# Attention and softplus MoE on one core: the row maxima of 15 of 16 head pairs turned by VectorE and placed by DMAs instead of turned by TensorE

## The chip, the cores and the metric

The kernel runs on one core of one Trainium2 chip. The time is device microseconds of that core, from a run without a profile; a profiled execution of the same kernel stands beside it. Engines are named as in the profile: PE (TensorE matmul), PEld (its weight loads), DVE (VectorE), ACT (ScalarE), POOL (GpSimd), SP (SyncE, which here only issues DMAs).

## What is computed

```python
def rotate(x):                       # x: 4 batches, 8 heads, 576 positions, 64 wide
    x1, x2 = (x[..., :half], x[..., half:])
    return np.concatenate([x1 * cos - x2 * sin, x1 * sin + x2 * cos], axis=-1)
q_rot, k_rot = (rotate(q), rotate(k))
scores = scale * np.matmul(q_rot, k_rot.transpose(0, 1, 3, 2))
scores = scores - np.max(scores, axis=-1, keepdims=True)
attn = np.exp(scores)
attn = attn / (np.sum(attn, axis=-1, keepdims=True) + 1e-09)
x = (attn @ v), heads side by side   # 2304 x 512
h = x @ w_in                         # 512 x 2048
g = np.maximum(h, 0.0) + np.log1p(np.exp(-np.abs(h)))
out = g @ w_out                      # 2048 x 512
```

All inputs are float32. The kernel splits each operand of a matmul into a high and a low part (`hl`, `kk`, `vs`, `ph` and `pl`, `wh` and `wl`) and adds up three products.

## The kernel before

Attention is done for 16 pairs of heads; the two heads of a pair lie on partitions 0 to 63 and 64 to 127, and every matmul comes twice, once for each half of the rows. The loop in `attention` runs over slots `s`, nine for a pair (`p, r = divmod(s, 9)`; slot r of a pair below). The order of the instructions on each engine is that in which the loop writes them (`pin`), and DMAs issued on SP keep theirs among themselves (`chain`). A slot holds work of several pairs:

- `p1(s)`, for pair p: scores with the queries on the partitions, 128 at a time against 288 keys, into a PSUM bank of the pool `ps_1`, which has one buffer; then DVE takes the negated row maximum of them into `mx` (L489). The last 64 queries of both heads, the corner, are done together, with `qd`, in which the two heads' queries stand in blocks off each other's rows; in all pairs but the first that is slot 5.
- `p2(n2)` with `n2 = s - 10`, so from slot 1 of the next pair on: the scores of the pair before again, now turned (keys on the partitions, 288 queries along the columns), into a bank of `ps_2`, which has two buffers. A fourth pair of matmuls adds the bias: a matrix of ones times `sm`, rows that hold the shift (minus the row maximum) of each query as a high and a low part. In slot 5 `p2c` does the corner keys with `kd`.
- `exps`: ACT takes the exponential twice, into `ph` and back into the bank; `low`: DVE forms `pl` from the two (L564). The loop keeps the bank that `low` used last as `spare`; free columns of it hold scratch values.
- `pv_half`: PE multiplies the probabilities with v, two slots later.

Between `p1` and `p2` the maxima, one to a partition, have to become rows. `shift0` (DVE) joins the two key halves after slots 6 and 8, `shift1` (POOL) makes high and low parts in `sh`, `shift2` (PE) turns them by matmuls with the unit matrix (L515: six in slot 0 of the next pair, for three groups of 128 queries, and four in slot 3), `shift3` (ACT, L522 and L526) copies them from PSUM into `sm`. `corner` copies the corner queries and keys into `qd` and `kd` with two DMAs each, in slots 1 and 8.

Beside this POOL and ACT turn the next pairs' queries and keys (`rope_steps`), and the MoE weights of three of sixteen chunks are converted early, in steps that `PLAN` and `MASKS` place; the steps of `MASKS` are two DVE instructions each (L136, L140) that use `spare`, two steps in slot 4 of twelve pairs. After slot 156 comes the MoE stage (`emit_h`, `emit_o`), 1152 and 864 matmuls and more, on PE without a gap.

Of the kernel before, what the change touches and what calls it, by code (L numbers as in the profile page):

```python
# [44 lines left out]
MASKS = {22 + 9 * n: n // 2 for n in range(12)}  # L45
# [10 lines left out]
def rope_attention_softplus_moe(  # L56
# [250 lines left out]
    def attention(es, es_r, es_s, tail, window, early):  # L307
# [8 lines left out]
        mask = at1.tile([128, 2], F32, name="mask")  # L316
# [15 lines left out]
        nc.vector.memset(sh[0].bitcast(F32), 0.0)  # L332
        flat = sh[0].rearrange("p c x -> p (c x)")
# [108 lines left out]
        order1 = ((*order1, None), (*order1[:5], None, *order1[5:]))  # L442

# [18 lines left out]
        def p1(n, between=None):  # L462
# [11 lines left out]
            if order1[p > 0][r]:  # L474
                c, j = order1[p > 0][r]
                to = m[:, j, c, :]
                for t, (a, b) in enumerate(terms):
                    for i, o in enumerate(rows):
                        pin(nc.tensor.matmul(out=sp[:, i, :HS], lhsT=q[o, a, c * 128:c * 128 + 128],  # L479
                                             rhs=k[o, b, j * HS:(j + 1) * HS], start=(t == 0), stop=(t == 2)))  # L480
            else:
                to = m[:, :, 4, 0]
# [68 lines left out]
        def exps(n, between=None):  # L551
# [3 lines left out]
            if between:  # L555
                between()
# [136 lines left out]
        def first(s):  # L693
# [5 lines left out]
            if n == 3:  # L699
                shift3(0, 1, x)  # L700
# [241 lines left out]
```

## Time and profile before

| | |
|---|---|
| median of 3 runs | 708.74 us (708.55 to 708.76) |
| profiled execution | 708.87 us, its span 706.8 us |
| PE, PEld busy | 698.1 us (99%), 649.3 us (92%) |
| DVE, ACT, POOL busy | 465.0, 388.0, 299.9 us |
| granted TensorE clock | 0.999 |
| attention ends, MoE begins (first `hp` matmul) | 301.2 us |

The span runs from the first to the last instruction. Busy time of PE includes the fill of the pipeline, since matmuls overlap; what a step costs PE is therefore read from the starts of its matmuls in the timeline, not from their durations. A wait is read from the idle time before an instruction and what ended it, and from the list of waits; a wait that ends on an engine with idle time after it costs nothing.

### The profile page before, as it was taken

Reading aid. Unit: us, or ns where it says so; the run is one execution under the profiler, and the core shown is the slowest. Engines: PE = TensorE matmul, PEld = TensorE weight load, DVE = VectorE, ACT = ScalarE, POOL = GpSimd, SP = SyncE. Lnnn points to the kernel's source line nnn. Section 1 sums busy time; section 2 is a strip of 40 time slices with the busy share of each in tenths; the row PEclk is TensorE's granted clock in tenths of the full one; section 3 lists DMA queues with packets and bytes.
Section 4 is the critical chain, followed back from the end, with each engine's and each line's share of the span. In section 5 each row is a group of like instructions: output and inputs, shape, how many; then the busy total and the mean of one; then the engine's idle time right before and its main releaser. Section 6 shows DMA issues by size and latency. Waiting matters only on the chain.

```text
span 706.8 us, 15573 instructions
## 1 busy us (share of the span) xinstructions
PE 698.1 (99%) x6275; PEld 649.3 (92%) x6275; DVE 465.0 (66%) x792; ACT 388.0 (55%) x751; POOL 299.9 (42%) x351
## 2 busy tenths in 40 slices
PE   8999999999999999999999999999999999999997
PEld 7899999999999999899999999999999999999996
DVE  6788888888888877669899894544543343444343
ACT  2788888888888887846766562322222222222222
POOL 7789899889988897820000000730500000000000
PEclk9999999999999999999999999999999999999999
DMA  7444344434454632024424330530100010001001
GB/s 265 147 113 142 112 141 115 141 112 143 138 166 137 167 102 65 19 70 129 138 93 131 108 95 2 177 92 1 68 0 1 1 45 1 1 1 45 1 1 45
DMA packets 40152, 61.33 MB, mean 87 GB/s; under 512 B 14288, under 2 KB 26896, under 8 KB 40080
## 3 DMA queue, kind: packets, MB, share of 16 engines
q1 hardware_dynamic: 37200, 55.16, 26.5%
q10 hardware_dynamic: 2880, 5.18, 2.0%
q8 instruction: 49, 0.80, 0.5%
q14 instruction: 23, 0.19, 0.1%
HBM read 48.64 MB, written 7.23 MB: 79 GB/s over the span
## 4 chain that ended last, share of the span: by engine, by line
PE 88%; DVE 4%; ACT 4%; DMA 2%; issue 1%; POOL 0%; SPq 0%; ACTq 0%; DVEq 0%
PE hp L235 29%; PE oa L274 14%; PE ob L274 14%; PE pv L597 13%; PE sp L549 9%; PE sp L479 6%; PE sp L451 3%; DVE pl L564 2%; ACT sp L557 2%; DVE mx L489 1%; ACT ph L554 1%; PE sp L515 1%; DMA tab<-cs 1%; DMA raw<-qk 0%; DVE sp L136 0%
## 5 line engine op out<-in xcount | busy, mean ns | idle before, releaser
L235 PE MATMUL hp<-x,wh 128*128 128x384 f32 x768 | 196.3, 336 | 0.0
L247 ACT ACTIVATE e<-e 128x384 f32<-128x384 f32 x96 | 50.4, 525 | 203.6 <-DVE e L245 196.5
L235 PEld LDWEIGHTS hp<-x,wh 128*128 128x128 f32 x768 | 140.7, 188 | 8.4 <-issue 0.2
L235 PE MATMUL hp<-x,wl 128*128 128x384 f32 x384 | 129.3, 337 | 0.0
L489 DVE TENSOR_REDUCE mx<-sp 128x2 f32<-128x576 f32 x144 | 108.3, 755 | 31.4 <-PE sp L479 24.3
L597 PE MATMUL pv<-ph,vs 64*128 64x288 f32 (+1 forms) x1152 | 125.2, 296 | 0.5 <-POOL vs L357 0.2
L564 DVE TENSOR_TENSOR pl<-sp,ph 128x576 fp32r<-128x576 f32 x144 | 108.3, 752 | 22.0 <-ACT sm L526 11.2
L554 ACT ACTIVATE ph<-sp 128x576 fp32r<-128x576 f32 x144 | 94.0, 653 | 41.8 <-PE sp L451 21.5
L245 DVE TENSOR_SCALAR e<-hp 128x384 int32<-128x384 int32 x96 | 53.4, 556 | 79.1 <-PE hp L235 79.1
L274 PE MATMUL oa<-wh,g 128*128 128x512 f32 x288 | 97.7, 393 | 0.0
L274 PE MATMUL ob<-wh,g 128*128 128x512 f32 x290 | 97.4, 391 | 0.0
L557 ACT ACTIVATE sp<-sp 128x576 f32<-128x576 f32 x144 | 93.0, 646 | 0.5
L597 PE MATMUL pv<-pl,vs 64*128 64x288 f32 x576 | 87.0, 292 | 0.2 <-DVE pl L564 0.2
L255 DVE TENSOR_TENSOR g<-m,g 128x384 fp32r<-128x384 f32 x96 | 55.8, 581 | 47.0 <-ACT g L252 46.9
L357 POOL TENSOR_TENSOR raw<-raw,tab 128x576 f32<-128x576 f32 x60 | 84.7, 1433 | 2.9 <-DMA raw<-qk 2.9
L250 DVE SCALAR_TENSOR_TENSOR m<-hp,e 128x384 f32<-128x384 f32 x96 | 53.5, 558 | 43.4 <-ACT e L247 42.1
L597 PEld LDWEIGHTS pv<-ph,vs 64*128 64x128 f32 (+1 forms) x1152 | 77.9, 158 | 3.0 <-PE pv L597 0.9
L549 PE MATMUL sp<-hl,kk 64*128 64x288 f32 x768 | 76.7, 302 | 1.1 <-DVE wc L140 0.9
L252 ACT CAST g<-m 128x384 fp32r<-128x384 f32 x96 | 49.3, 513 | 48.6 <-DVE m L250 45.8
L479 PE MATMUL sp<-kk,hl 64*128 64x288 f32 x768 | 73.7, 294 | 0.5 <-DVE kk L357 0.3
L235 PEld LDWEIGHTS hp<-x,wl 128*128 128x128 f32 x384 | 72.0, 188 | 0.0
L274 PEld LDWEIGHTS ob<-wh,g 128*128 128x128 f32 x290 | 54.4, 188 | 10.3
(112 smaller groups left out, 1052.6 us busy)
## 6 DMA issues: line engine op xcount, KB each, us to landing
raw<-qk SPq DMA_DIRECT2D x29, 576.0 KB
wraw<-w SPq DMA_DIRECT2D x23, 512.0 KB
vf<-v SPq DMA_DIRECT2D x16, 320.0 KB
wraw<-w SPq DMA_DIRECT2D x14, 256.0 KB
x<-xt SPq DMA_DIRECT2D x32, 72.0 KB
xd<-xt SPq DMA_DIRECT2D x32, 72.0 KB
x<-rd SPq DMA_DIRECT2D x16, 144.0 KB
out<-wc ACTq DMA_DIRECT2D x9, 256.0 KB
```

Source lines behind the costliest of these rows:

```text
L235: pin(nc.tensor.matmul(out=hp, lhsT=a[f][:, c * 128:(c + 1) * 128], rhs=piece(j, c)[:, b, :], start=(i == 0), stop=(i == 11),))
L250: pin(nc.vector.scalar_tensor_tensor(out=m, in0=hp, scalar=0.0, in1=e, op0=ALU.max, op1=ALU.add))
L255: pin(nc.vector.tensor_tensor(out=g[:, 1, :], in0=m, in1=g[:, 0, :].bitcast(F32), op=ALU.subtract))
L274: pin(nc.tensor.matmul(out=po[:, z], lhsT=g[:, s, t * 128:(t + 1) * 128], rhs=b[f][:, 512 + z.start:512 + z.stop], start=(first and i == 0 ...
L357: pin((nc.vector if e == "V" else nc.gpsimd).tensor_tensor(out=out, in0=in0, in1=in1, op=op))
L479: pin(nc.tensor.matmul(out=sp[:, i, :HS], lhsT=q[o, a, c * 128:c * 128 + 128], rhs=k[o, b, j * HS:(j + 1) * HS], start=(t == 0), stop=(t = ...
L489: pin(nc.vector.tensor_reduce(out=to, in_=sp[:, :, :HS], axis=AX.X, op=ALU.max, negate=True))
L549: pin(nc.tensor.matmul(out=sp[:, i, :HS], lhsT=lhs, rhs=rhs, start=(t == 0), stop=(t == 3)))
L554: pin(nc.scalar.activation(out=ph, in_=sp, func=AF.Exp, scale=D ** -0.5))
L557: pin(nc.scalar.activation(out=sp, in_=sp, func=AF.Exp, scale=D ** -0.5))
L564: pin(nc.vector.tensor_tensor(out=pl, in0=sp[:, :, :HS], in1=ph.bitcast(F32), op=ALU.subtract))
L597: two.append(pin(nc.tensor.matmul(out=pv[:k, i, :HS], lhsT=lhs, rhs=x[o, j if c is None else i, :], start=first, stop=last)))
```

## The change

In all pairs but for the first three groups of pair 0, `shift` does the work of `shift0` to `shift3`. DVE joins the key halves twice, into a scratch place in `spare` and, rounded, into `st`; subtracts for the low part; and turns `st` in blocks of 32 by 32 into `turned`. Then SP issues four DMAs that carry rows of 32 from there to partitions 62 to 65 of `sm` (high and low part, two heads), and two more for a corner. `sm` is cleared once at the start.

The corner queries of pairs 1 to 15 are now queries 256 to 319, not the last 64 (`places`), so the first group of shifts (0 to 319, ready after slot 5) covers the first half of the queries, and the second (320 to 575) is ready after slot 8. `corner` copies with two POOL instructions instead of two DMAs, but for pair 0. The mask steps go from two in slot 4 to one in slot 3 and one in slot 4, and the loads of v from slot 6 to slot 7. The DMAs of a group stand on SP behind the instruction that they wait for, and ahead of the next pair's loads.

```diff
-MASKS = {22 + 9 * n: n // 2 for n in range(12)}
+MASKS = {21 + 9 * n + i: n // 2 for n in range(12) for i in range(2)}
...
-        sh = [at1.tile([128, 5, 128], F32R, name=f"sh{i}") for i in range(2)]
-        sm = [at1.tile([128, 5, 128], F32R, name=f"sm{i}") for i in range(2)]
+        sh = at1.tile([128, 3, 128], F32R, name="sh")
+        sm = [at1.tile([128, S], F32R, name=f"sm{i}") for i in range(2)]
         mx = [at1.tile([128, 2, 5, 2], F32, name=f"mx{i}") for i in range(2)]
-        sf = at1.tile([128, 6, 2], F32, name="sf")
+        st = at1.tile([128, 5, 32], F32R, name="st")
+        turned = [at1.tile([128, 3 - i, 32], F32, name=f"tu{i}") for i in range(2)]
...
-        nc.vector.memset(sh[0].bitcast(F32), 0.0)
-        flat = sh[0].rearrange("p c x -> p (c x)")
+        nc.vector.memset(sh.bitcast(F32), 0.0)
+        for x in (*sm, st):
+            nc.vector.memset(x.bitcast(F32), 0.0)
+        flat = sh.rearrange("p c x -> p (c x)")
...
+            t = t[:, :, 256:320] if p and i == 0 else t[:, :, 512:576]
             for n, o in enumerate(rows):
                 m = 64 * ((n + i) % 2)
-                keep(queue.dma_start(out=x[o, :, m:m + 64].bitcast(F32), in_=t[o, :, 512:].bitcast(F32)))
+                if p:
+                    rnd(x[o, :, m:m + 64], t[o].bitcast(F32), "P")
+                else:
+                    keep(queue.dma_start(out=x[o, :, m:m + 64].bitcast(F32), in_=t[o].bitcast(F32)))
...
+        places = (((0, 0), (128, 1), (256, 2), (384, 3), (512, 4)), ((0, 0), (128, 1), (320, 3), (448, 4), (256, 2)))
...
-        def shift0(p, g):
-            m, cs, to = mx[p % 2], slice(3 * g, 3 + 2 * g), slice(3, 6, 2) if g else slice(0, 3)
-            pin(nc.vector.tensor_reduce(out=sf[:, to], in_=m[:, :, cs].rearrange("p j c a -> p c a j"), axis=AX.X,
-                                        op=ALU.min))
+        def shift(p, g):
+            cs, n = slice(3 * g, 3 + 2 * g), turned[g]
+            m, x = mx[p % 2][:, :, cs].rearrange("p j c a -> p c a j"), st[:, cs]
+            parts = x[:, :, 0:4].rearrange("p c (a h) -> p c a h", h=2)
+            full = spare[0][:, 1, HS:HS + 2 * (3 - g)].rearrange("p (c a) -> p c a", a=2)
+            for to in (full, parts[:, :, :, 0]):
+                pin(nc.vector.tensor_reduce(out=to, in_=m, axis=AX.X, op=ALU.min))
+            tt(parts[:, :, :, 1], full, parts[:, :, :, 0].bitcast(F32), ALU.subtract, "V")
+            pin(nc.vector.transpose(out=n, in_=x.bitcast(F32)))
+            to = sm[p % 2].bitcast(F32)
+            starts = {at: c for c, at in places[p > 0][:4] if cs.start <= at < cs.stop}
+            c0 = min(starts.values())
+            for k in range(4):
+                at = to[62:66, c0:c0 + 128 * len(starts)].rearrange("p (c x) -> p c x", x=128)
+                chain(nc.sync.dma_start(out=at[:, :, 32 * k:32 * k + 32], in_=n[32 * k:32 * k + 4, :len(starts)]))
+            c0 = places[p > 0][4][0]
+            for h in range(2 * (len(starts) < cs.stop - cs.start)):
+                chain(nc.sync.dma_start(out=to[62 + h:66 + h:2, c0:c0 + 64], in_=n[h::32, len(starts)]))
...
-        def shift1(p, g):
-            cs = slice(3 * g, 3 + 2 * g)
-            if g:
-                tt(sf[:, 4, :], sf[:, 5, 0:1].to_broadcast([128, 2]), mask, ALU.mult, "P")
-            x = sh[p % 2].rearrange("p c (a x) -> p c a x", a=2)
-            rnd(x[:, cs, :, 0], sf[:, cs], "P")
-            tt(x[:, cs, :, 1], sf[:, cs], x[:, cs, :, 0].bitcast(F32), ALU.subtract, "P")
-
-        def shift2(p, g, t):
-            for n, c in enumerate((3, 4) if g else range(3)):
+        def shift2(t):
+            for c in range(3):
                 for i, o in enumerate(rows):
-                    pin(nc.tensor.matmul(out=t[:, i, HS + n * 64:HS + n * 64 + 64], lhsT=sh[p % 2][o, c, :],
+                    pin(nc.tensor.matmul(out=t[:, i, HS + c * 64:HS + c * 64 + 64], lhsT=sh[o, c, :],
                                          rhs=identr[o, o], start=True, stop=True))
-            return t[:, :, HS:HS + (128 if g else 192)]
-
-        def shift3(p, g, x):
-            cs = slice(3, 4) if g else slice(0, 3)
-            w = 64 if g else 192
-            pin(nc.scalar.copy(out=sm[p % 2][:, cs, :].rearrange("p c (t x) -> p t c x", t=2),
-                               in_=x[:, :, :w].rearrange("p t (c x) -> p t c x", x=64)))
-            if g:
-                for i, o in enumerate(rows):
-                    pin(nc.scalar.copy(out=sm[p % 2][o, 4, :64], in_=x[o, i, 64:]))
...
-                g = {0: 0, 3: 1}.get(r) if s <= NSLOT + 3 else None
-                x = None if g is None else shift2(p - 1, g, ps2[n2])
                 if r == 5 and s < NSLOT:
                     p1(s, lambda flip, after=(): p2c(n2, flip, after))
                 else:
                     p2(n2)
-                exps(n2, None if g != 0 else (lambda: shift3(p - 1, g, x)))
-                if g == 1:
-                    shift3(p - 1, g, x)
...
-                elif r in (6, 8) and s != 6:
-                    shift0(p, r // 8)
...
             if s in MASKS:
-                for _ in range(2):
-                    next(early[MASKS[s]])
-            if r == 7 and PER < s < NSLOT:
-                shift1(p, 0)
-            if r == 0 and 0 < s <= NSLOT:
-                shift1(p - 1, 1)
+                next(early[MASKS[s]])
+            if r in (5, 8) and 5 < s < NSLOT:
+                shift(p, r // 8)
...
-                if r == 6 and p + 1 < NP:
+                if r == 7 and p + 1 < NP:
                     load_v(p + 1)
```

Where it moves instructions, three places. PE at the beginning of slot 0 of a pair, before:

```order
L597 MATMUL pv<-ph,vs_133 64x288 x2
L597 MATMUL pv<-pl,vs_133 128x288 x2
L515 MATMUL sp_1155<-identr,sh_123 128x64 [waits DVE_49,Pool_49]
L515 MATMUL sp_1155<-identr,sh_123 128x64 x5
L549 MATMUL sp_1155<-hl,kk_100 128x288 x6
L549 MATMUL sp_1155<-sm_126,ones 128x288 x2
```

and after:

```order
L601 MATMUL pv<-ph,vs_133 64x288 x2
L601 MATMUL pv<-pl,vs_133 128x288 x2
L555 MATMUL sp_1164<-hl,kk_100 128x288 [waits DVE_49]
L555 MATMUL sp_1164<-hl,kk_100 128x288 x5
L555 MATMUL sp_1164<-sm_124,ones 128x288 x2
```

The six turning matmuls are gone, and the wait for POOL with them. PE one slot later, at the first `p2` of the next pair (`sp` is the bank, `sm` the shift rows), before:

```order
L549 MATMUL sp_1201<-hl,kk_101 128x288 [waits DVE_49]
L549 MATMUL sp_1201<-hl,kk_101 128x288 x5
L549 MATMUL sp_1201<-sm_125,ones 128x288 [waits Activation_49]
L549 MATMUL sp_1201<-sm_125,ones 128x288
L597 MATMUL pv<-ph,vs_133 128x288 x2
```

and after:

```order
L555 MATMUL sp_1200<-hl,kk_101 128x288 [waits DVE_49]
L555 MATMUL sp_1200<-hl,kk_101 128x288 x5
L555 MATMUL sp_1200<-sm_123,ones 128x288 [waits DMAHW5_49,DMAHW6_49,DMAHW2_49,DMAHW7_49,DMAHW1_49,DMAHW0_49]
L555 MATMUL sp_1200<-sm_123,ones 128x288
L601 MATMUL pv<-ph,vs_133 128x288 [waits Activation_49]
```

The bias matmul waits for the landing of six DMAs where it waited for ACT's copies. DVE from the `low` of slot 4 to that of slot 6, in a pair with mask steps, before:

```order
L564 TENSOR_TENSOR pl<-sp_1725,ph 128x576 [waits Activation_49]
L136 TENSOR_SCALAR sp_1725<-wc 128x128 [waits DVE_49]
L140 SCALAR_TENSOR_TENSOR wc<-wraw,sp_1725 128x128 [waits DMAHW0_49,DVE_49]
L136 TENSOR_SCALAR sp_1725<-wc 128x128 [waits DVE_49]
L140 SCALAR_TENSOR_TENSOR wc<-wraw,sp_1725 128x128 [waits DVE_49]
L489 TENSOR_REDUCE mx_127<-sp_1769 128x2 [waits PE_49]
L564 TENSOR_TENSOR pl<-sp_1768,ph 128x576 [waits Activation_49]
L489 TENSOR_REDUCE mx_127<-sp_1843 128x2 [waits PE_49]
L493 TENSOR_REDUCE sf<-mx_127 128x6 [waits DVE_49,Pool_49]
L564 TENSOR_TENSOR pl<-sp_1818,ph 128x576 [waits Activation_49]
```

and after:

```order
L568 TENSOR_TENSOR pl<-sp_1319,ph 128x576 [waits Activation_49]
L136 TENSOR_SCALAR sp_1319<-wc 128x128 [waits DVE_49]
L140 SCALAR_TENSOR_TENSOR wc<-wraw,sp_1319 128x128 [waits DVE_49]
L497 TENSOR_REDUCE mx_126<-sp_1363 128x2 [waits PE_49]
L568 TENSOR_TENSOR pl<-sp_1362,ph 128x576 [waits Activation_49]
L505 TENSOR_REDUCE sp_1362<-mx_126 128x6 [waits DVE_49]
L505 TENSOR_REDUCE st<-mx_126 128x3x2
L359 TENSOR_TENSOR st<-sp_1362,st 128x3x2 [waits DVE_49]
L507 STREAM_TRANSPOSE tu_128<-st 128x96 [waits DMAHW5_49,DMAHW2_49,DMAHW6_49,DMAHW1_49,DMAHW7_49,DMAHW0_49,DVE_49]
L497 TENSOR_REDUCE mx_126<-sp_1446 128x2 [waits PE_49]
L568 TENSOR_TENSOR pl<-sp_1421,ph 128x576 [waits Activation_49]
```

One mask step stands behind slot 4's `low` instead of two, and the four instructions of the shift stand between slot 5's `low` and slot 6's maximum; the scratch place of the first is in the bank (`sp_1362`) that this `low` has read.

## Rows read from the trace of the kernel before

**Rows 1.** The page, busy us (share of the span) and instructions of engines:
```profile
PE 698.1 (99%) x6275; PEld 649.3 (92%) x6275; DVE 465.0 (66%) x792; ACT 388.0 (55%) x751; POOL 299.9 (42%) x351
```
**Rows 2.** Busy time by stretch, one per pair, fourteen pairs; clock, DMA share, GB/s last:
```profile
133.49:150.99 17.50, 17.50 (x262) 17.12 (x258) 14.32 (x24) 14.97 (x30) 15.71 (x18) 1.00 0.50 144
...
sum 247.45, PE 245.93 PEld 239.88 DVE 199.86 ACT 208.68 POOL 221.17; mean PE 17.57 PEld 17.13 DVE 14.28 ACT 14.91 POOL 15.80
```
**Rows 3.** Timeline of PE, slot 0's `p2` with six turning matmuls (start, us, form):
```profile
123.69 0.42 PE L515 MATMUL sp<-identr,sh 64*128 64x64 f32 x6
...
124.42 0.31 PE L549 MATMUL sp<-sm,ones 64*128 64x288 f32 x2
```
**Rows 4.** Timeline of PE, slot 3's `p2` with four turning matmuls:
```profile
129.19 0.31 PE L515 MATMUL sp<-identr,sh 64*128 64x64 f32 x4
...
129.80 0.31 PE L549 MATMUL sp<-sm,ones 64*128 64x288 f32 x2
```
**Rows 5.** Timeline of PE: slot 6's `p2`, then slots 0 and 1 of the next pair:
```profile
135.46 0.66 PE L549 MATMUL sp<-hl,kk 64*128 64x288 f32 x6
135.95 0.30 PE L549 MATMUL sp<-sm,ones 64*128 64x288 f32 x2
...
142.47 0.56 PE L479 MATMUL sp<-kk,hl 64*128 64x288 f32 x6
...
143.27 0.56 PE L549 MATMUL sp<-hl,kk 64*128 64x288 f32 x6
143.66 0.30 PE L549 MATMUL sp<-sm,ones 64*128 64x288 f32 x2
...
144.19 0.57 PE L479 MATMUL sp<-kk,hl 64*128 64x288 f32 x6
```
**Rows 6.** Waits of the whole span: waiting, waited for, us in total, times, longest:
```profile
PEld sp L549 <- DVE wc L140: 3.7, 12, 0.5
```
**Rows 7.** Timeline of DVE, slots 4 to 6 and 8 to 0; idle before in brackets:
```profile
135.11 0.29 DVE L140 SCALAR_TENSOR_TENSOR wc<-wr,sp 128x128 int32<-128x128 int32 x1
...
135.99 0.75 DVE L564 TENSOR_TENSOR pl<-sp,ph 128x576 fp32r<-128x576 f32 x1
137.48 0.76 DVE L489 TENSOR_REDUCE mx<-sp 128x2 f32<-128x576 f32 x1 [0.75 <-PE sp L479]
...
141.95 0.75 DVE L564 TENSOR_TENSOR pl<-sp,ph 128x576 fp32r<-128x576 f32 x1
143.07 0.76 DVE L489 TENSOR_REDUCE mx<-sp 128x2 f32<-128x576 f32 x1 [0.37 <-PE sp L479]
```
**Rows 8.** Timeline of DVE, pair 0's first shift, two instructions that depend on each other:
```profile
16.59 0.17 DVE L499 TENSOR_REDUCE sp<-mx 128x6 f32<-128x12 f32 x1
16.80 0.17 DVE L354 TENSOR_SCALAR sh<-sp 128x6 fp32r<-128x6 f32 x1
```
**Rows 9.** Groups by line and shape: count, busy us, mean ns, idle before:
```profile
L354 POOL TENSOR_SCALAR kk<-raw 128x576 fp32r<-128x576 f32 x13 | 8.9, 684 | 1.1
...
L136 DVE TENSOR_SCALAR sp<-wc 128x128 int32<-128x128 int32 x24 | 7.1, 295 | 0.8
...
L354 POOL TENSOR_SCALAR sh<-sf 128x4 fp32r<-128x4 f32 x16 | 3.2, 199 | 1.4
...
L218 POOL TENSOR_SCALAR x<-xm 128x192 fp32r<-128x192 f32 x4 | 1.4, 355 | 0.4
```
**Rows 10.** Instructions of L435: shortest, median, longest ns, first and last start:
```profile
L435 SPq DMA_DIRECT2D qd<-hl x32: 591/640/1081, 10.8 to 266.6; - x32
```
**Rows 11.** Timeline of SP and POOL, last sums; SP waits for `xs`, POOL for `rc`:
```profile
303.24 0.59 SPq L624 DMA_DIRECT2D xs<-xt  x1
...
304.94 0.33 SPq L631 DMA_DIRECT2D rc<-xs  x1
...
306.88 0.34 POOL L634 TENSOR_SCALAR rc<-rc 128x36 f32<-128x36 f32 x1 [2.27 <-DMA rc<-xs]
```
**Rows 12.** Instructions of L451 from 131 to 134 us: the waits of PE's sequencer:
```profile
L451 PEldq EVENT_SEMAPHORE  x2: 51/51/51, 131.5 to 132.8; - x2
```

More of the change, by code (lines that the diff above doesn't have):

```diff
@@ L315, in attention @@
         onesd = at1.tile([128, 128], F32R, name="onesd")
-        mask = at1.tile([128, 2], F32, name="mask")
         rp1 = pool(es_r, "rp1", 1, "right")
@@ L475, in p1 @@
                 c, j = order1[p > 0][r]
-                to = m[:, j, c, :]
+                c, at = places[p > 0][c]
+                to = m[:, j, at, :]
                 for t, (a, b) in enumerate(terms):
                     for i, o in enumerate(rows):
-                        pin(nc.tensor.matmul(out=sp[:, i, :HS], lhsT=q[o, a, c * 128:c * 128 + 128],
+                        pin(nc.tensor.matmul(out=sp[:, i, :HS], lhsT=q[o, a, c:c + 128],
                                              rhs=k[o, b, j * HS:(j + 1) * HS], start=(t == 0), stop=(t == 2)))
             else:
-                to = m[:, :, 4, 0]
+                to = m[:, :, places[p > 0][4][1], 0]
                 ends = between and between(0)
@@ L502, in shift01 @@
             tt(x[:, 0:3, :, 1], t, x[:, 0:3, :, 0].bitcast(F32), ALU.subtract, "V")
[L504 to L513 removed]
+        def shift2(t):
+            for c in range(3):
                 for i, o in enumerate(rows):
[L515 removed]
+                    pin(nc.tensor.matmul(out=t[:, i, HS + c * 64:HS + c * 64 + 64], lhsT=sh[o, c, :],
                                          rhs=identr[o, o], start=True, stop=True))
[L517 to L526 removed]
+            pin(nc.scalar.copy(out=sm[0][:, :384].rearrange("p (c t x) -> p t c x", t=2, x=64),
+                               in_=t[:, :, HS:HS + 192].rearrange("p t (c x) -> p t c x", x=64)))
         def tile2(n):
@@ L533, in p2c @@
             p = n // PER
-            q, bias = hl_t[p, 0], sm[p % 2].rearrange("p c x -> p (c x)")
+            q, bias = hl_t[p, 0], sm[p % 2]
             return crossed(ps2[n], [*(kd[:, b, :] for _, b in terms), onesd], [*(q[:, a, :] for a, _ in terms), bias],
@@ L540, in p2 @@
             q, k = hl_t[p, 0], hl_t[p, 1]
-            sp, bias = ps2[n], sm[p % 2].rearrange("p c x -> p (c x)")
+            sp, bias = ps2[n], sm[p % 2]
             if r == 4:
@@ L549, in p2, with exps @@
                     pin(nc.tensor.matmul(out=sp[:, i, :HS], lhsT=lhs, rhs=rhs, start=(t == 0), stop=(t == 3)))
-        def exps(n, between=None):
+        def exps(n):
             sp = ps2[n][:, :, :HS]
@@ L554, in exps @@
             pin(nc.scalar.activation(out=ph, in_=sp, func=AF.Exp, scale=D ** -0.5))
-            if between:
-                between()
             pin(nc.scalar.activation(out=sp, in_=sp, func=AF.Exp, scale=D ** -0.5))
@@ L654, in attention @@
         nc.gpsimd.memset(ones.bitcast(F32), 1.0)
-        nc.gpsimd.memset(mask, 0.0)
         for x in (onesd, qd, kd):
@@ L659, in attention @@
             nc.gpsimd.memset(onesd[o, 64 - 64 * i:128 - 64 * i].bitcast(F32), 1.0)
-            nc.gpsimd.memset(mask[o, i:i + 1], 1.0)
         for i in range(2):
@@ L663, in attention @@
             nc.gpsimd.memset(vs[i][:, :, :, 1, :].bitcast(F32), 1.0)
-        nc.gpsimd.memset(sh[1].bitcast(F32), 0.0)
         load_v(0)
@@ L695, in first @@
             tile2(n)
-            x = shift2(0, 1, ps2[n]) if n == 3 else None
             p2(n)
             exps(n)
-            if n == 3:
-                shift3(0, 1, x)
         for s in range(NSLOT + LAG + PVD + 1):
@@ L718, in attention @@
                     p2(n2)
-                exps(n2, None if g != 0 else (lambda: shift3(p - 1, g, x)))
-                if g == 1:
-                    shift3(p - 1, g, x)
+                exps(n2)
             elif LAG - 2 <= s < LAG:
@@ L743, in attention @@
             if s == LAG - 4:
-                shift3(0, 0, shift2(0, 0, wp))
+                shift2(wp)
             if s >= LAG and s in FIRST:
```

2 lines of the change are left out of this document (1 added, 1 removed).

## The prediction

> **What bounds the kernel now.** I read the page's busy times first: PE is busy 99% of the span [rows 1]. A busy PE alone proves little, so next came the table by stretches, cut at each pair's first corner matmul of slot 5. Fourteen pairs fill 27.5 to 275 us, 17.68 us each, at full clock; of that PE is busy 17.57, DVE 14.28, ACT 14.91, POOL 15.80 [rows 2]. So attention is PE's, POOL stands closest behind, and the MoE stage after it (which the change leaves alone) starts when PE is through with attention. What is taken off PE in a pair comes off the total, until another engine or a wait is the next limit. In PE's timeline two matmuls on the two row halves take 0.13 us, and a `p2` needs 0.39 us from its first matmul to its bias matmuls (143.27 to 143.66) [rows 5]. Every longer step is either extra work or a wait.
>
> **The change part by part.** Times are set against the profiled execution, 708.87 us (span 706.8 plus 2.1 around it); the median of the three runs is 708.74, so a saving is taken from either.
>
> *Turning on PE (gain).* With six turning matmuls ahead of it, slot 0's `p2` takes 123.69 to 124.42, 0.73 us to its bias matmuls; with four, slot 3's takes 129.19 to 129.80, 0.61 [rows 3, 4]. Against 0.39 that is 0.34 and 0.22, and both are on the path, since PE waits for nothing there. Fifteen pairs lose the six and sixteen the four (pair 0 keeps its six): 15 x 0.34 + 16 x 0.22 = 8.6 us. The ACT copies that followed go too; ACT and DVE have idle time in these slots, so I count nothing for them.
>
> *Mask steps (gain).* Two steps (four DVE instructions) stand behind slot 4's `low` and work in the bank that `low` has just read. The last ends at 135.40, and slot 6's `p2`, which needs that bank, starts at 135.46 [rows 5, 7]. The waits list has it 12 times, 3.7 us, on the weight loads [rows 6]; after such a wait the same six matmuls also need 0.49 instead of 0.39 (135.46 to 135.95) [rows 5], 1.2 us more in twelve. Upper bound 4.9. Weight loads run one pair ahead of the matmuls, so PE itself may lose 0.13 less each time: lower bound 3.3. I take 3.9. With one step in slot 3 and one in slot 4, the bank comes free a step, some 0.65 us, earlier (134.75 for 135.40), so I count the whole wait as gone.
>
> *Shift on DVE (loss).* Per group: two reductions, a subtraction, a transpose, and one reduction goes. Small dependent DVE instructions start 0.21 us apart (16.59, 16.80) [rows 8]. The transpose has no row: by the trace it lies between a six-element instruction's 0.17 and the 0.295 of a 128-column one [rows 8, 9]; 96 columns are nearer to the latter, 0.25. Together about 0.8 us. In slot 5 the DVE idles from 136.74 to 137.48 [rows 7], which hides it. In slot 8 it idles only 0.37 us after `low` (142.70 to 143.07) [rows 7]. There DVE would be free at about 143.45; slot 0's scores, ready 0.34 us earlier than now, at 143.03 - 0.34 = 142.69, wait, and their maximum ends at 144.2. The next `p1`, which needs that bank, would be due at 144.19 - 0.34 = 143.85 [rows 5]. So PE waits some 0.3 us per pair, 15 x 0.3 = 4.5 us. Bounds: nothing (if DVE has caught up by slot 8) and 0.6 (if slot 5 does the same), 9.0 us. Below nothing I exclude: four instructions come to this place and one small one leaves it.
>
> *Placing by DMA.* Counted at nothing if the rows land in time; what hides it is the stretch of five slots from slot 5 to the next pair's slot 1. In the trace slot 5's `low` ends at 136.74 and the first bias matmuls of that pair come at 143.66 [rows 5, 7]: 6.92 us, of which the change takes 0.34 (turning) and 0.24 (the wait of slot 6, here 0.15 + 0.09), leaving 6.3. Out of that: shift on DVE 0.8; six issues on SP, the last of them five issues behind the first, at the 0.64 us that a `qd` issue takes [rows 10] 3.2 us; then the landing. `xs` was issued at 303.24 and SP, which waited for it, issued the read at 304.94: 1.7 us; POOL had that read's data at 306.88: 1.94 [rows 11]. 0.8 + 3.2 + 1.94 = 5.9, so 0.4 us is left. Slots 3 and 4's DMAs have a slot more, with four issues. Nothing on the path, but with a thin cover (below). Behind the waiting DMAs SP now holds the next `raw`, `vf` and weight loads, which go out some 8 us later than before; `raw`'s query half is needed only in the next pair's slot 3, and `vf` in its slot 5, so none of them is late.
>
> The Trainium skill (DMA: Bandwidth & Descriptors, Anatomy of one DMA and Rules for kernel authors) speaks against ten DMAs of 1 KB: a fixed cost near 2.0 us each, on the GpSimd path, and advice to merge anything under 64 KB. With 2.0 for the landing the cover would be 0.3 us instead of 0.4, and the sum would be the same. The trace's 1.7 to 1.94 agrees with it.
>
> *Corner copies on POOL.* Four of 64x128 replace four DMAs, and five small instructions (0.20 us each, 1.0) go. Rows: 0.36 us for 192 columns, 0.69 for 576 [rows 9], so 0.30 for 128 columns, 1.2 together: 0.2 us more per pair on an engine with 1.9 us to spare (1.1 in a shorter pair of 17.1). Nothing.
>
> *The rest.* Two more zero fills on DVE at the start lie in the wait for the tables. Pair 0's shift and its six DMAs come in the start-up, where PE has gaps anyway: plus or minus 0.5, not counted.
>
> Sum: 8.6 + 3.9 - 4.5 = 8.0 us saved: 700.9 in a profiled execution, **700.7** as the median. Its own ends: 8.6 + 4.9 - 0 = 13.5 (695.3) and 8.6 + 3.3 - 9.0 = 2.9 (705.8).
>
> **The rivals.**
>
> *The rows land too late (slower).* The place is the first bias matmul of a pair, which waits for six landings; PE takes its work in order, so a late row stops everything. With p the time from issue to issue, the wait is 0.8 + 5p + 1.94 - 6.3 per pair. It begins at p = 0.71, and from 0.82 on it costs more than the 0.53 us per pair that is saved. At p = 0.9 it is 0.94 x 15 = 14 us: 714.8. For it: one `qd` issue took 1.08 [rows 10], and the destinations are single partitions, of which no row is seen. Against it: the median of 32 such issues is 0.64, and SP has nothing else to do at that time.
>
> *POOL becomes the bound (little gain).* If a corner copy costs as much as a full 576-column one, 0.69 [rows 9], POOL's busy time grows by 4 x 0.69 - 1.0 = 1.7 to 17.5 us per pair, and PE can't go below that: 14 x 0.18 = 2.5 us saved, 706.2. Against it: 192 columns already cost half of 576.
>
> *PE pays for its waits (little gain).* Six landings before one matmul and four before another mean eight extra wait instructions of 51 ns [rows 12] per pair. Standing in the stream they cost 0.41 us, 6.1 in all: 706.8. Against it: one of the two waits of slot 5's corner matmuls was run at 131.5, the other at 132.8 [rows 12], so the sequencer gets waits out of the way early when what they wait for is there.
>
> *The change doesn't do what it says.* The order of the instructions shows the turning matmuls gone in all pairs but the first group, and one mask step in each of the two slots, so this can only fail in a slot that I did not read.
>
> **How the numbers follow.** A measurement can tell about 0.2%, 1.4 us, from no change. Forecast (695.3 to 705.8, most likely 700.7): 0.70. Late rows (from 707 up, mostly over 710): 0.14. POOL: 0.07. Waits on PE: 0.07. Something else on either side: 0.02. Faster: 0.70 plus nearly all of POOL's and two thirds of the waits' share, 0.83; within 0.2%: 0.05; slower 0.12. For the range I leave out most of the late rows' share and a little at the lower end: 695.3 to 706.8.
>
> **What would show it.** In the profile after: pairs of 17.1 us (17.0 to 17.3) by the same cut; no turning matmuls past the first 20 us; no wait of slot 6's `p2` for a mask step; a wait of slot 1's `p1` for slot 0's maximum of some 0.3 us; and no wait of bias matmuls for a DMA. If PE's waits name the rows' DMAs, the first rival holds. If POOL's busy time per pair reaches PE's, the second. If small gaps stand before the bias matmuls though the DMAs have landed, the third. If DVE's transposes take far over 0.3 us, the DVE term was too small.

## The result, and the profile after

The changed kernel is slower: 713.14 us (711.17 to 714.42, four runs) against 708.67 (708.55 to 708.76), a ratio of 1.006 (95% interval 1.0042 to 1.0078). The forecast was 700.7, and 695.3 to 706.8 for the range. The profiled run took 714.42 us, its span 712.6.

The first row of the page answers [rows 1], the stretches between the pairs' first `qd` matmuls answer [rows 2]. The page:

```profile
PE 695.0 (98%) x6121; PEld 642.0 (90%) x6121; DVE 479.1 (67%) x888; ACT 370.8 (52%) x688; POOL 301.5 (42%) x329
```

Stretches of the changed kernel (us; PE, PEld, DVE, ACT, POOL busy; clock, DMA share, GB/s):

```profile
81.59:98.95 17.36, 17.36 (x252) 16.62 (x250) 15.24 (x31) 13.80 (x26) 15.32 (x16) 1.00 0.32 93
98.95:117.67 18.72, 17.40 (x250) 16.58 (x248) 15.48 (x32) 14.07 (x26) 17.09 (x19) 1.00 0.48 147
...
189.39:206.71 17.32, 17.32 (x248) 16.60 (x249) 15.24 (x31) 13.80 (x26) 15.41 (x17) 1.00 0.43 121
206.71:228.75 22.04, 18.75 (x251) 18.13 (x250) 16.20 (x32) 14.08 (x26) 17.93 (x18) 0.92 0.55 165
...
sum 252.46, PE 243.58 PEld 233.64 DVE 211.96 ACT 193.32 POOL 221.83; mean PE 17.40 PEld 16.69 DVE 15.14 ACT 13.81 POOL 15.84
```

The pairs alternate. Every second one takes 16.9 to 17.4 us, close to the forecast of 17.1 and below the 17.68 of before; the ones between, up to 228.75, take 18.1 to 18.7, and one 22.0. In those PE is idle for 0.8 us and more, where no stretch of before has more than 0.4. The list of waits names the place (waiting, waited for, us in total, times, longest):

```profile
PEld pv L601 <- ACT xt L612: 9.0, 7, 3.5
PEld sp L487 <- DVE mx L497: 4.2, 21, 0.4
...
ACT wc L144 <- DMA wraw<-w: 4.7, 3, 3.0
...
ACT wc L144 <- DMA wr<-w: 2.6, 2, 1.4
```

The wait of [rows 6] (slot 6's `p2` for a mask step) is gone. In its place PE waits for ACT to empty the one `pv` bank, and ACT waits for a DMA: the load of an early weight chunk's second half. One such place on three engines; SP first:

```profile
103.20 2.83 SPq L513 DMA_DIRECT2D sm<-tu  x4
106.13 1.15 SPq L516 DMA_DIRECT2D sm<-tu  x2
107.38 0.33 SPq L344 DMA_DIRECT2D raw<-qk  x1
107.81 0.39 SPq L425 DMA_DIRECT2D vf<-v  x1
108.25 0.46 SPq L635 DMA_DIRECT2D rc<-xs  x1
108.76 0.42 SPq L855 DMA_DIRECT2D wr<-w  x1
```

ACT:

```profile
111.37 0.64 ACT L561 ACTIVATE sp<-sp 128x576 f32<-128x576 f32 x1
113.23 0.43 ACT L144 ACTIVATE wc<-wr 128x256 f32<-128x256 f32 x1 [1.22 <-DMA wr<-w]
113.57 0.62 ACT L612 COPY xt<-pv 65x576 f32<-65x576 f32 x1
```

PE:

```profile
112.36 0.66 PE L487 MATMUL sp<-kk,hl 64*128 64x288 f32 x6
114.24 0.54 PE L601 MATMUL pv<-ph,vs 64*128 64x288 f32 x4 [1.21 <-ACT xt L612]
```

SP takes its queue in order. It stood at the shift's DMAs until DVE had turned the rows (103.2), spent 4 us on the six issues, and only then issued `raw`, `vf`, `rc` and, at 108.76, the weights. ACT wanted them at 112.0 (behind the 0.64 of 111.37) and had them at 113.23; ACT also works in order, so the `xt` copy behind stood still with it, and so did PE. In the kernel before, the load at the same place of a pair goes out 13.3 us ahead of its conversion, which runs without a wait:

```profile
133.52 0.47 SPq L866 DMA_DIRECT2D wr<-w  x1
...
146.84 0.42 ACT L144 ACTIVATE wc<-wr 128x256 f32<-128x256 f32 x1
```

In the changed kernel 3.3 us were left up to the moment when ACT wanted the data (108.76 to 112.0), and the load took 4.5 us to land. (The expectation of `queue_late` below sets 11.5 against the 3.3; it counts the kernel before only to the first half's conversion.)

### The profile page after: what moved, and what is told of

Its sections match the earlier page's. It is cut to its first block, busy times and chain, and to the rows that moved or that the text cites. A ratio compares the mean times of both kernels' runs of the same rounds, so it can differ in the third digit from the quotient of the medians.

```text
span 712.6 us, 15564 instructions
## 1 busy us (share of the span) xinstructions
PE 695.0 (98%) x6121; PEld 642.0 (90%) x6121; DVE 479.1 (67%) x888; ACT 370.8 (52%) x688; POOL 301.5 (42%) x329
## 4 chain that ended last, share of the span: by engine, by line
PE 87%; DMA 3%; POOL 3%; DVE 2%; ACT 2%; issue 1%; SPq 0%; ACTq 0%; DVEq 0%; POOLq 0%
PE hp L235 28%; PE oa L274 14%; PE ob L274 14%; PE pv L601 13%; PE sp L555 7%; PE sp L487 6%; PE sp L458 4%; POOL raw L359 2%; DMA wr<-w 1%; DMA tab<-cs 1%; DVE mx L497 1%; ACT ph L560 1%; DMA wraw<-w 1%; POOL hl L359 1%; DVE pl L568 1%
## 5 line engine op out<-in xcount | busy, mean ns | idle before, releaser
L487 PE MATMUL sp<-kk,hl 64*128 64x288 f32 x768 | 77.0, 304 | 1.2 <-ACT kk L353 0.4
L555 PE MATMUL sp<-hl,kk 64*128 64x288 f32 x768 | 74.2, 297 | 0.3 <-DVE st L359 0.3
L487 PEld LDWEIGHTS sp<-kk,hl 64*128 64x128 f32 x768 | 57.6, 186 | 7.0 <-DVE mx L497 4.2
```

What stands on the lines that cost most here:

```text
L487: pin(nc.tensor.matmul(out=sp[:, i, :HS], lhsT=q[o, a, c:c + 128], rhs=k[o, b, j * HS:(j + 1) * HS], start=(t == 0), stop=(t == 2)))
L555: pin(nc.tensor.matmul(out=sp[:, i, :HS], lhsT=lhs, rhs=rhs, start=(t == 0), stop=(t == 3)))
```

## The experiments

The length of a pair below is the mean of the 13 stretches between the `qd` matmuls from pair 2's to the last, 17.66 us before and 17.99 after. All times are medians; before was 708.56 to 708.73 on the same chips.

**The weight load, from four sides.** Theory A: the loss is the late load. Rivals: the small DMAs (B), the shift on DVE (C). First the load alone, moved ahead of the shift (`load_early`):

```diff
-LOADS = {13 + 3 * (i % 2) + 18 * (i // 2): divmod(i, 4) for i in range(14)} | {
+LOADS = {12 + (i % 2) + 18 * (i // 2): divmod(i, 4) for i in range(14)} | {
```

> The changed kernel with one number edited: the two halves of an early weight chunk are loaded in slots 3 and 4 of the pair instead of 4 and 7, so on SP's queue the second half stands ahead of the shift's DMAs, raw and vf instead of behind them. Theory A (the second half lands late, ACT's first conversion of it blocks ACT, the xt copy behind it comes late, and PE waits for the single pv bank in every second pair): the stalls at pv go, all pairs take 17.1 to 17.4 us, and the time is 701 to 704 us. Theory B (the small DMAs themselves, their landing or the traffic they bring, cost the time): nothing changes, 711 to 714. Theory C (the shift on DVE costs PE more than 0.3 us in each pair): the alternation of pairs goes at most in part, 706 or more.

705.73 us (0.9958 of before, 0.9943 to 0.9973): 7.4 us come back and the alternation is gone (16.97 to 17.51 us from pair 2 on; the stretch of 18.6 ahead of them stays, so its cause is another). The list of waits:

```profile
PEld sp L487 <- DVE mx L497: 3.9, 19, 0.4
...
PEld pv L601 <- ACT xt L612: 0.6, 2, 0.4
```

A stands, but the time is 2 us above what it foretold: something else is left. Next, SP as it was and only the reader moved (`conv_late`):

```diff
-                    for do, o in (*steps[:2], (None, parts[0]), (None, parts[1]), *steps[2:], (None, parts[2]),
+                    for do, o in (steps[0], (None, parts[0]), (None, parts[1]), *steps[1:], (None, parts[2]),
```

and slot number 20 in `PLAN` becomes 24.

> The changed kernel with SP's order left as it is, but ACT's conversion of the second half of a weight chunk moved from slot 2 to slot 6 of the next pair (its two mask steps on the first half stay in slots 3 and 4). The load goes out as late as before, and only its reader moves by some 7.8 us. Theory A: the xt copy no longer stands behind a conversion that waits for its data, the stalls at pv go as with the earlier load, 701 to 704 us. If the late order on SP costs something else as well (raw, vf, or traffic in that stretch), 706 to 711. Theory B: 711 to 714.

705.69 us, the same gain. So it is not the queue's order as such, or its traffic, that costs the time, but the conversion that waits in ACT's order ahead of `xt`. Then the reverse, the kernel before with late loads (`queue_late`): the DMAs of `raw`'s query half and of `vf` stand behind slot 8's store, and

```diff
-LOADS = {13 + 3 * (i % 2) + 18 * (i // 2): divmod(i, 4) for i in range(14)} | {
+LOADS = {13 + 4 * (i % 2) + 18 * (i // 2): divmod(i, 4) for i in range(14)} | {
```

> The kernel before, with nothing of the change in it: raw's query half, vf and the second half of a weight chunk are issued behind slot 8's store instead of in slots 5, 6 and 7, so that the weight load goes out some 3.3 us ahead of its conversion, as it does in the changed kernel, instead of 11.5. Theory A: the same stall at pv, 1 to 2 us in every second pair, 6 to 7 of them: 715 to 721 us. Theory B and theory C: no shift DMAs and no shift on DVE, so 708.7 within 1 us.

710.10 us: slower (1.0013 to 1.0034), but by 1.4, not 6. ACT waited 1.7 us in all. The load went out 5.3 us ahead of its conversion (106.62 to 111.89), not 3.3, and takes about 5 to land behind `raw` and `vf`: I had not asked how long it takes. The miss is one of lead, as the next run shows, with the load behind the two `qd` copies too (`queue_later`, `6 * (i % 2)` in place of 4, for the last chunk 4).

> As queue_late, with the second half of the weight chunk one place further back on SP: behind the two qd copies too, some 1.4 us later (the last chunk but one place less). Queue_late was only 1.4 us slower than before; there ACT waited 0.3 to 0.7 us for the load and PE 2.6 us in all for pv. Theory A: every further 0.1 us of the load comes through to PE, six times 1.2 to 1.4 us more than queue_late: 717 to 719, with waits of ACT for the load of 1.5 to 2.2 us. If queue_late's 1.4 us came from raw and vf and not from the weight load: 710 to 711.

715.43 us, 5.3 more for 1.4 us of lead, though less than the 717 to 719 expected. Its waits stand beside those of the changed kernel above:

```profile
PEld pv L597 <- ACT xt L608: 8.9, 9, 2.4
...
ACT wc L144 <- DMA wraw<-w: 5.7, 4, 2.2
...
ACT wc L144 <- DMA wr<-w: 1.9, 2, 1.2
```

The kernel before, with none of the shift's DVE work and none of its DMAs, loses 6.9 us, nearly as much as the change did. Last, the early load in the kernel before (`early_alone`, the edit of `load_early`):

> The kernel before with the earlier weight load alone. Theory A: there the load was never late, so nothing changes, 708.6 within 0.7. If the earlier load is a gain of its own: 703 to 707.

708.66 us: the early load is no gain of its own. The 7.4 us belong to the change.

**What the removed work was worth.** `load_early` saves 3.0 us where the forecast had 8.0. In it PE has three short waits in a pair that before has not; means over the 13 pairs, from the starts of matmuls: 0.11 us at slot 7's `p1`, 0.15 at slot 1's `p2`, 0.29 at slot 3's `p1`. `noshift`, on top of `load_early` like all that follow but `masks_only`, leaves the whole shift out:

```diff
-            if r in (5, 8) and 5 < s < NSLOT:
-                shift(p, r // 8)
```

> The kernel with the earlier weight load (705.7 us), with the whole shift of pairs 1 to 15 and of pair 0's second group left out, DVE's part and the DMAs: the bias rows stay at what was there, so the softmax is not shifted. There PE's stretch between two pairs' first qd matmuls is 17.29 us, with three waits that the kernel before has not: 0.11 us at slot 7's p1, 0.15 at slot 1's p2, 0.29 at slot 3's p1. Theory D: the first two are the price of the shift on DVE, the third is not (there PE now comes to slot 3's p1 before DVE has read slot 2's scores, since the turning matmuls that stood between are gone). Then pairs of 17.03 us and 701.8 us (701 to 703), with the wait at slot 3's p1 as before. Rival: all three are the shift's, pairs of 16.7 and 697.4 us (696.5 to 699). Rival: the shift costs nothing on DVE's side, 705.7.

701.55 us, 17.08 us a pair. Slot 1's wait is gone and slot 3's stays, as expected; slot 7's stays for the most part too (0.08), which was not (`masks_back` below takes it away). The 13 pairs give 2.7 of the 4.2 us; the rest lies outside them (below). PE there, in `noshift`, where 0.13 us is the step from the two bias matmuls on, and 0.40 that of six:

```profile
109.80 0.33 PE L555 MATMUL sp<-sm,ones 64*128 64x288 f32 x2
110.07 0.66 PE L487 MATMUL sp<-kk,hl 64*128 64x288 f32 x6
110.64 0.53 PE L601 MATMUL pv<-ph,vs 64*128 64x288 f32 x4
```

0.27 and 0.57 instead. The chain is PE's `p1` of slot 2, DVE's maximum of it (0.75 us), and slot 3's `p1` into the same single bank; between the two `p1` PE has only one half of a `pv` and one `p2`. Four useless matmuls put back there (`refill3`) should then be free:

```diff
                 else:
+                    for c in range(2 if r == 3 and s <= NSLOT + 3 else 0):
+                        for i, o in enumerate(rows):
+                            pin(nc.tensor.matmul(out=ps2[n2][:, i, HS + c * 64:HS + c * 64 + 64], lhsT=sh[o, c, :],
+                                                 rhs=identr[o, o], start=True, stop=True))
                     p2(n2)
```

> The kernel with the earlier weight load, with four 64-column matmuls of no use put back ahead of slot 3's p2, where the second group's turning matmuls stood. In the kernel before, these took 0.22 us of a pair. Theory D: they fill a time in which PE would wait for slot 2's maximum, so they cost nothing: 705.7 within 0.9. If the prediction's gain in slot 3 is real, they cost 15 times 0.22: 709.0.

705.35 us: they are free (17.29 a pair, as without). The second group's turning matmuls had filled a wait. The same with six ahead of slot 0's `p2` (`refill0`):

```diff
+                    for c in range(3 if r == 0 and s <= NSLOT + 3 else 0):
```

> The kernel with the earlier weight load, with six 64-column matmuls of no use put back ahead of slot 0's p2, where the first group's turning matmuls stood. By the prediction's term they cost 15 times 0.34: 710.8. If part of that gain is given back at slot 1's p2 (0.15 us a pair), they fill that wait too: 15 times 0.19, 708.6. If all of it was given back, as in slot 3: 705.7.

707.69 us, 2.0 more: of slot 0's 5.1 us some 2.0 were left. A pair takes 17.47, 0.18 more, and slot 1's wait is gone, so in the pairs the partial reading (0.19) holds. The mask steps, both put back in slot 4 (`masks_back`), and, the other way, split in the kernel before (`masks_only`, the same edit reversed):

```diff
-MASKS = {21 + 9 * n + i: n // 2 for n in range(12) for i in range(2)}
+MASKS = {22 + 9 * n: n // 2 for n in range(12)}
...
-                next(early[MASKS[s]])
+                for _ in range(2):
+                    next(early[MASKS[s]])
```

> The kernel with the earlier weight load, with both mask steps put back in slot 4. The prediction's term for splitting them is 3.3 to 4.9 us, so 709.0 to 710.6. Alone in the kernel before, the split cost 4.1 us, and its trace shows why: slot 3's pl comes late behind ACT's copies of the turned rows, and the step behind it holds the bank that slot 5 needs. If the split is a loss in every kernel, 701.6; if it is a gain as soon as those copies are gone, 709 to 711.

> The kernel before with one part of the change alone: one mask step in slot 3 and one in slot 4 instead of two in slot 4. By the prediction's term the wait of slot 6's p2 goes, 3.3 to 4.9 us: 704.8 (703.8 to 705.4). If another wait ends last in that place (the exponentials on ACT), less than 1 us: 707.7 to 708.7.

`masks_back` took 704.98 us, 0.75 less, with pairs as long (17.28): the split earned nothing, and the 0.75 is no more than the runs of `load_early` differ among themselves (705.26 to 706.26). Slot 6's wait came back (2.9 us in the list), but slot 7's `p1` and slot 5's corner matmuls lost theirs. `masks_only` took 712.84 us (1.0043 to 1.0073), 4.1 lost where 3.9 were forecast to be won. DVE and PE there:

```profile
205.78 0.76 DVE L564 TENSOR_TENSOR pl<-sp,ph 128x576 fp32r<-128x576 f32 x1 [0.69 <-ACT sm L526]
206.58 0.29 DVE L136 TENSOR_SCALAR sp<-wc 128x128 int32<-128x128 int32 x1
206.91 0.29 DVE L140 SCALAR_TENSOR_TENSOR wc<-wraw,sp 128x128 int32<-128x128 int32 x1
```

```profile
206.58 0.30 PE L597 MATMUL pv<-pl,vs 64*128 64x288 f32 x2
207.29 0.67 PE L451 MATMUL sp<-hl,kd 64*128 64x288 f32 x6 [0.41 <-ACT sp L557]
```

`pl` of slot 3 waits for ACT's copies of turned rows, the mask step follows it, and slot 5 needs that bank: PE starts there 0.71 us after the two matmuls before began (0.13 is usual), in each such pair. (The row names ACT, which was done at 206.98; what ended last was DVE, at 207.20.)

**What the shift costs.** `dve_only` leaves out the shift's DMAs alone:

```diff
-                chain(nc.sync.dma_start(out=at[:, :, 32 * k:32 * k + 32], in_=n[32 * k:32 * k + 4, :len(starts)]))
...
-                chain(nc.sync.dma_start(out=to[62 + h:66 + h:2, c0:c0 + 64], in_=n[h::32, len(starts)]))
```

> The kernel with the earlier weight load (705.7 us), with the shift's DVE instructions left as they are and its DMAs left out (the bias rows aren't placed, so the softmax is not shifted). Theory: the ten small DMAs of a pair cost nothing themselves, 705.7 within 0.8. If their landing or traffic held something up, as the first rival of the prediction has it, down to 701.6, the time without any shift.

703.47 us: by the medians the DMAs cost 2.3 of the shift's 4.2 us, and DVE 1.9. In the profiled runs 0.6 us of the 2.3 are in the 13 pairs (17.25 for 17.29) and 0.7 at the end of attention, where the bias matmuls do wait for a landing (0.5 us, once). The rest isn't shown to be theirs: 0.4 us lie ahead of the first of these DMAs, and 0.6 behind the first `hp` matmul, a stretch that is 0.5 us longer than before in `masks_only` too, which has none of them, and only 0.1 in the `hybrid` below, which has six in a pair. Could DVE's part stand elsewhere? `shift_mid` moves it between maximum and `pl` of slots 6 and 0, and its full minima to SBUF:

```diff
-            full = spare[0][:, 1, HS:HS + 2 * (3 - g)].rearrange("p (c a) -> p c a", a=2)
+            full = sf[:, cs]
...
-            if r in (5, 8) and 5 < s < NSLOT:
-                shift(p, r // 8)
...
+                if r == 6 and s > 6:
+                    shift(p, 0)
+            if r == 0 and 0 < s <= NSLOT:
+                shift(p - 1, 1)
```

> The kernel with the earlier weight load, with the shift's DVE instructions moved from behind the pl of slots 5 and 8 to between maximum and pl of slots 6 and 0, so that they hold up a pl, which has two banks, and not a maximum, which has one. (The full minima go to SBUF instead of a spare piece of PSUM, and the rows go out some 1 to 1.5 us later.) Theory D: the waits at slot 7's p1 and slot 1's p2 go, 17.03 us a pair, 701.8 us (701 to 703.5). If the pl becomes what ends last, or the first group's rows now come late to slot 1's bias matmuls, 705.7 or more.

726.09 us. That was two changes, so each was run alone: the place (`mid_psum`: `full = bank[:, 1, HS:...]`, where `bank` is `ps2[n2]`), and the home of the minima (`sbuf_full`: the first hunk alone).

> The kernel with the earlier weight load, with the shift between maximum and pl of slots 6 and 0 as in shift_mid, the full minima now in a spare piece of the PSUM bank of that slot's own scores. If the place is good and the rows come in time: 701.8 (701 to 703). By the starts in the trace the last of the first group's rows would land 0.8 us later than now (107.9 instead of 107.1), where the bias matmul that needs them would be due at 107.55: then PE waits some 0.35 us there in each pair and the gain is lost, 705 to 708, with bias matmuls waiting for DMAs. Near 726 the place alone would be at fault in shift_mid.

> The kernel with the earlier weight load (705.7 us), with the shift's full minima kept in SBUF instead of a spare piece of PSUM, and nothing else. If a subtraction with both inputs in SBUF has to wait for the GpSimd instruction that is running, it takes 0.4 to 1.0 us instead of 0.164, the maxima of slots 6 and 0 come later by 0.2 to 0.8 us, and PE waits for them: 710 to 720 us. If the home of the operand makes no difference: 705.7 within 0.8.

`mid_psum`: 717.69 us, more than expected. Waits of the matmuls there:

```profile
PE sp L555 <- DMA sm<-tu: 7.3, 12, 1.1
PE sp L555 <- issue: 1.4, 3, 0.5
```

This is the prediction's first rival, reached by 1.1 us of delay: DVE's maximum of slot 6 stands idle 0.47 us for its scores, which I had left out. Of the 0.87 us that a pair is longer (18.16), 0.66 come at slot 1's bias matmuls, which is the delay less the 0.46 us by which the rows were early in `load_early`, and 0.28 at slot 8's `p2`, which waits for slot 6's `pl`. `sbuf_full`: 705.32 us, so the home alone costs nothing, and my 710 to 720 was wrong; the 8.4 us between `shift_mid` and `mid_psum` come from both together (the subtraction, last section).

**A better version.** `hybrid`: the early load, both mask steps in slot 4, the first group as in the change, and the second group turned on PE again in slot 3, where four matmuls are free (a minimum on DVE in slot 8, rounding on POOL in slot 0, one ACT copy).

```diff
+                    if r == 3 and p > 1 and s <= NSLOT + 3:
+                        turn(ps2[n2])
                     p2(n2)
+                x = ps2[n2]
                 exps(n2)
+                if r == 3 and p > 1 and s <= NSLOT + 3:
+                    turned1(p - 1, x)
```

> A version drawn from the runs so far: the earlier weight load, both mask steps in slot 4, the first group by DVE and DMAs as in the change, but the second group of pairs 1 to 15 turned on PE in slot 3 again, where four such matmuls cost nothing (one DVE minimum in slot 8, two small POOL instructions in slot 0, four matmuls and one ACT copy in slot 3). It takes some 0.6 us of DVE out of slot 8 of a pair and four DMAs. If slot 1's wait (0.15 us a pair) goes and nothing comes for it: 705.0 less 2.3, 702.7 (702 to 703.5). If ACT's copy in slot 3 delays what stands behind it: 705 or more.

703.04 us, as expected, 0.9925 of before (0.9910 to 0.9940), with 17.12 us a pair: faster than the kernel before and than the change. With the mask steps split (`hybrid_split`), which puts an ACT copy ahead of slot 3's `pl` again:

> The hybrid (703.0 us) with the mask steps split over slots 3 and 4 again. It has one ACT copy of turned rows in slot 3 (the kernel before has three). If such copies are what made the split a loss, slot 5's corner matmuls wait for the bank of slot 3 again, by about the length of the copy, some 0.3 us in the pairs with a step, 12 times, while slot 6's wait of 0.2 us goes: 703 to 706, and the waits list names slot 5. If the copy doesn't matter: 703.0 within 0.7, and no wait in slot 5.

707.83 us, 4.8 more, beyond the range, and the waits name slot 5:

```profile
PEld sp L460 <- ACT sp L575: 4.2, 11, 0.5
```

So the split is a loss where an ACT copy stands in slot 3, and about nothing where none does. `hybrid_c1` copies pair 1's corners by DMAs:

```diff
-                if p:
+                if p > 1:
                     rnd(x[o, :, m:m + 64], t[o].bitcast(F32), "P")
```

> The hybrid with the corners of pair 1 alone copied by DMAs, as in the kernel before; the other pairs' stay on GpSimd. There, in the hybrid, four copies (0.67 and 0.67 us) stand ahead of a vs that PE waits for some 2 us; in the kernel before PE waits 0.6 us at that place. If these copies are what is late: 1.0 to 1.5 us less, 701.5 to 702.0. If POOL is held by something else (it waited 3.2 us for ACT before): 703.0 within 0.5.

702.94 us, no change: PE's wait for `vs` went from 2.0 to 1.3 us, and a wait for a `qd` copy (0.5) and one for a maximum (0.8) came. What the first pairs lose against before, from pair 0's first `qd` matmul to pair 2's, stays open: 1.1 us in `load_early` (27.83 for 26.76) and 1.5 in `hybrid`.

## Why the prediction was wrong

*The step that failed* is the sentence on SP's queue: "`raw`'s query half is needed only in the next pair's slot 3, and `vf` in its slot 5, so none of them is late". The delay was about right (forecast some 8 us; in the places shown above the load went out 0.03 us after its pair's first `qd` matmul before and 9.8 after), and the weight loads stood in the sentence, but no reader was looked up for them. Their reader is ACT in slot 2, and behind it in ACT's order stands `xt`. Of 13.3 us of lead 3.3 were left, less than the 4.5 of the landing. That is 7.4 us, against 0 in the sum.

*The sum otherwise.* The runs make a chain: 708.7 before, 701.55 without any shift (and the load early), 705.73 with it, 713.14 with the late load.

| term | forecast | measured | by |
|---|---|---|---|
| turning and mask wait, together | -12.5 | -7.2 | `noshift` |
| of it slot 3's turning | -3.5 | 0 | `refill3` |
| of it slot 0's turning | -5.1 | -2.0 | `refill0` |
| of it the mask steps | -3.9 | +0.75 | `masks_back` |
| shift on DVE and DMAs | +4.5 and 0 | +1.9 and +2.3 (1.3 of it placed) | `dve_only` |
| late loads | 0 | +7.4 | `load_early` |

`noshift` keeps all of the change but the shift, so its row holds the start too: of `load_early`'s 3.0 us the 13 pairs give 4.8, and the first pairs take 1.1 back, where the prediction left plus or minus 0.5 uncounted. The parts of the first row, each undone alone with the shift in place, come to 1.3 us and not to 7.2. That each fills a wait which another leaves is seen at slots 1, 3, 5 and 7; that this is the whole difference is not shown, since no run undoes them together.

*Turning* was costed rightly as PE's time (0.34 and 0.22 a pair; the matmuls' starts before show 0.56 in all), and wrongly as the path's: "both are on the path, since PE waits for nothing there". In slot 3 PE waited for nothing because the turning filled the time. What was late next, DVE's maximum of the slot before, was not asked.

*The mask wait* did go (0.31 us a pair by the starts). But a step in slot 3 stands ahead of slot 4's maximum on DVE, and the gain came back as waits in slots 5 and 7, which `masks_back` does not have.

*The shift on DVE* was sized well as DVE's time, not as the path's (1.9 us for 4.5): a transpose of 96 columns took 0.28 us, one of 64 took 0.25, a group some 0.8. In the changed kernel, against [rows 7]:

```profile
102.27 0.18 DVE L505 TENSOR_REDUCE sp<-mx 128x6 f32<-128x12 f32 x1
102.35 0.16 DVE L505 TENSOR_REDUCE st<-mx 128x6 fp32r<-128x12 f32 x1
102.54 0.17 DVE L359 TENSOR_TENSOR st<-sp,st 128x6 fp32r<-128x6 f32 x1
102.86 0.28 DVE L507 STREAM_TRANSPOSE tu<-st 128x96 f32<-128x96 f32 x1
103.06 0.72 DVE L497 TENSOR_REDUCE mx<-sp 128x2 f32<-128x576 f32 x1
```

Its wait was put at slot 1's `p1`, 0.3 us a pair; it came at slot 1's `p2`, 0.15.

*Placing by DMA*: the rival of late rows did not happen within the pairs. The issues took 0.64 us, as in [rows 10]. By the semaphores that the bias matmuls wait for, a DMA had landed 1.8 us after its issue began (1.5 for those of a corner; medians in `load_early`), close to the 1.7 to 1.94 of [rows 11]; the rows of the first group were there 0.46 us before their reader (median of the pairs; forecast 0.4; in one pair only 0.1), and `mid_psum` shows the price beyond. At the end of attention one landing did come late. The Trainium skill's fixed cost near 2.0 us (DMA: Bandwidth & Descriptors, Anatomy of one DMA) is stated for DMAs that GpSimd issues; these, issued by SP, took 1.5 and 1.8.

*POOL's corner copies* took 0.295 us each, as estimated (0.30); POOL bounds no pair. (The rival's price was added up wrongly: 4 x 0.69 - 1.0 is 1.76, so 17.56 us a pair and 707.0, not 706.2.) *The zero fills* on DVE at the start are three more, not two, 1.3 us together; pair 0's first `qd` matmul came no later for them (18.62, before 18.66). *Waits on PE*: no such gaps stand before the bias matmuls.

## What to carry to other kernels

When a DMA that waits for a result goes into an in-order queue, list every transfer behind it, look up the reader of each, and compare the lead that is left with the landing time; then ask what stands behind that reader on its own engine. Work taken off the busiest engine is worth its time only until the next round trip (here matmul, maximum, matmul into one bank) is as long as what is left between; a few useless matmuls put back in that place tell what it was worth. A move that costs 4 to 5 us in one kernel (the split of the mask steps) can cost next to nothing in another in which one neighbour is gone, so parts of a change are best priced with the rest in place.

## What was not expected of the hardware

The long stall at 220 us cost more than its own 3.6 us. Stretches of the changed kernel around it (PE alone is of interest, and the clock, third from the end):

```profile
216.00:220.40 4.40, 4.40 (x66) 4.24 (x66) 3.99 (x7) 2.92 (x6) 3.99 (x7) 1.00 0.88 233
220.40:224.00 3.60, 0.38 (x6) 0.14 (x4) 1.18 (x2) 0.94 (x3) 3.60 (x4) 1.00 0.46 131
224.00:228.00 4.00, 3.93 (x36) 3.90 (x38) 2.22 (x5) 2.62 (x6) 1.95 (x2) 0.58 0.80 260
228.00:232.00 4.00, 4.00 (x64) 4.00 (x62) 2.67 (x6) 2.05 (x5) 0.41 (x1) 0.99 0.02 3
```

After 3.6 us in which PE did 0.38 us of work, the granted clock was 0.58 over 4 us, which is mostly the lower level of 1.2 GHz, and PE did 36 matmuls there instead of the 64 of the next 4 us: some 1.7 us more. The other four stops of PE for `xt`, 0.8 to 1.3 us, had no such sequel. In `queue_later` it came twice, after stops of 2.1 us (0.68 over the next 4.2) and of 1.8 (0.73 from 226 to 230 us), but in `hybrid` a stop of 1.8 us was followed by the full clock. The changed kernel's runs spread over 3 us, those of before over 0.2; the two slowest of its four (714.42 and 713.40) list a mean clock of 0.998 and 0.997, the others 1.000. With those others (712.88 and 711.17) the late load costs 7.2 and 5.4 us, so the fall of the clock is only a part of the 7.4.

The subtraction of the shift takes 0.164 us with one input in PSUM (0.161 to 0.166 in the 31 cases of `load_early`). With both in SBUF it took 0.37 (median, `sbuf_full`) and up to 1.36 (`shift_mid`), and where it was slow it ended some 20 ns after the GpSimd instruction that was running when it began:

```profile
L360 DVE TENSOR_TENSOR st<-sf,st x31: 166/533/1364, 22.2 to 299.9; 128x4 fp32r<-128x4 f32 x16, 128x6 fp32r<-128x6 f32 x15
```

The Trainium skill (SBUF — State Buffer, SBUF: two separate sides) says that a DVE instruction with two SBUF inputs and a GpSimd instruction that reads SBUF exclude each other for their whole length; the trace agrees.
